# First chunks of the hidden layer with four weight blocks, and unit 0's rows of xT by DMA

## The chip, the cores and the metric

The kernel runs on one NeuronCore of a Trainium2 chip. The metric is device time in microseconds, lower is better. TensorE (PE) multiplies, VectorE (DVE), ScalarE (ACT) and GpSimd (POOL) work element by element, and SyncE (SP) issues most DMAs. Each engine runs its instructions in the order of the program and waits on semaphores for the others. 16 DMA engines move data between HBM and the on-chip memory (SBUF); matmuls write to PSUM.

## The reference

An RWKV6 attention is followed by a feed-forward layer. B, H, S, D = 4, 8, 768, 48; 3072 tokens, a model width of 384 and a hidden width of 2048. The two weight matrices are given in double precision.

```python
for t in range(S):
    cur = np.einsum('bhd,bhe->bhde', u[None] * kt, vt)
    y[:, :, t] = np.einsum('bhd,bhde->bhe', rt, state + cur)
    state = wt[:, :, :, None] * state + np.einsum('bhd,bhe->bhde', kt, vt)
...
x = np.ascontiguousarray(attn_out.transpose(0, 2, 1, 3)).reshape(B * S, H * D)
h = x @ w_in
sp = np.maximum(h, 0.0) + np.log1p(np.exp(-np.abs(h)))
g = h * erf(sp)
return (g @ w_out).astype(np.float32)
```

## The kernel before

**Steps and units.** Twelve steps s each take 128 tokens of two batches through the attention; the result of a step is a unit of 256 tokens for the feed-forward layer. Each step multiplies within its chunk by levels: at level n products of k and r (`level_products`, L728) are masked into the tile `own`, and VectorE then scales k and r by products of the decay w (`scale`, L375; L368 in step 0) before the next level. After six levels `from_own` (L772) and `through_state` (L798) sum y in PSUM. While the levels of step s run, PE fills the gaps with matmuls of earlier units: `hidden` (x @ w_in, L1289) and `project` (g @ w_out). `place` is called after each level and puts one piece of such work there. A piece of `hidden` is six matmuls of 256 columns (two chunks of 128 hidden columns, times three blocks of xT); a profile counts 12 records for them. A copy (L1298) takes each piece's result out of PSUM, from one of two buffers `ps_m`. So piece n + 2 can begin only when the copy of piece n is done.

**The three blocks of xT.** y has four groups of 128 partitions, each with two heads of 48 rows in halves of 64. 384 rows fit into three full blocks: groups 0 to 2 give rows 0 to 47 of each half, and the fourth group's 2 x 48 rows are spread, 16 by 16, over the spare rows 48 to 63 of the three blocks, which the text calls lanes. The fourth group is first copied to SBUF (`y3`, L807). For the steps from 1 on, the three groups are copied to xT (L828) and six small DMAs of 16 partitions carry y3's rows into the lanes (L834), three on SP's queue and three on ScalarE's. Step 0 is done otherwise: `hop` multiplies y3 with three constant matrices `apart` (L816, built at L1672 to L1678), which adds the rows to the lanes of y in PSUM, and ScalarE copies the sums to xT (L822). `hop` stands between the two halves of level 1's products in step 1.

**The weights.** They come as double-precision words and are made into single precision on the chip, two chunks at a time; number i means the i-th such pair, 0 to 7 for w_in. l(i) loads the words in two halves (`load`, L181), b(i) takes the high words on ScalarE (L291), r(i) the low ones (L299), h(i) shifts on VectorE (L308), and o(i) adds on GpSimd (L321). From pair 2 on, b(i) writes into the PSUM tile y, so it must wait for h(i - 1). The words have three buffers, so l(i) waits for r(i - 3). The loads share SP's queue with the inputs of the steps and are held back by hand. A copy of one column into the words' buffer (L274 on ScalarE, L276 on GpSimd) waits for something that is to come first, and the DMA waits for the copy. l(1) is opened by the totals of step 0, l(2) by `middle`, l(3) by y3, l(4) by the last block of xT. In step 1, h(i) stands on VectorE in front of the scaling at L375: `stages["h"](level + 1)`, then `scale(s, level)`.

**Order on the engines.** It is written by hand in `attend_first` (step 0) and `attend` (the others); ScalarE's copy `fence` (L781) stands between the two passes of `from_own`. In step 1, place 2 issues step 2's first input (L1720) and w. ScalarE multiplies that input by u (L452) before b(7), and copies level 6's products to `own` (L745) after r(7).

## Time and profile before

| what | us |
|---|---|
| runs of the kernel | 569.4 median of 3 (568.28 to 569.9) |
| the profiled execution | 567.75, with a span of 566.0 |
| PE busy in the span | 560.9 |
| VectorE, ScalarE, GpSimd busy | 453.0, 358.3, 241.4 |
| first three steps' waits of ScalarE for weight loads (L291) | 3.0 in 3 |
| shift products of `hop` (L816) | 1.56, from 22.19 |
| copies of unit 0 to xT (L822) | 0.90, from 23.91 |

All other times are microseconds from the start of the span in the profiled execution. An engine's line in the timeline gives start, duration, engine, line of the kernel, operation, tile written from tiles read, count, and in brackets the idle time ahead of it with what ended it. "PEld" is the loading of weights into the array, "SPq" and "ACTq" are DMA issues by those engines. The chain of waits is followed back from the last instruction, at each step to what released it.

### The profile page before, as it was taken

What the parts mean: (1) busy time and instruction counts of PE and PEld (TensorE: products, weight loads), DVE (VectorE), ACT (ScalarE), POOL (GpSimd) and SP (SyncE); (2) the same over time, 40 slices, a digit from 0 to 9 for tenths busy, and PEclk for the clock granted to TensorE, in tenths of its full rate; (3) what the DMA queues carried; (4) which work ended last, traced back from release to release, by engine and by line L of the source; (5) the groups of instructions that cost most, each with busy time, mean ns of one, the idle gap of its engine ahead of it and who ended that gap; (6) DMA issues with size and microseconds to landing.
All of it is one profiled execution on the core that took longest, in us unless ns stands there. A gap on an engine that the chain in (4) does not pass through costs nothing.

```text
span 566.0 us, 16708 instructions
## 1 busy us (share of the span) xinstructions
PE 560.9 (99%) x7316; PEld 500.7 (88%) x7316; DVE 453.0 (80%) x512; ACT 358.3 (63%) x495; POOL 241.4 (43%) x262
## 2 busy tenths in 40 slices
PE   9999999999999999999999999999999999999997
PEld 6788886588988998998998998998899899989997
DVE  8895986999899898898798789689689487477910
ACT  4687787556558858748757766765676771589500
POOL 3875482533885883393284185176072000000000
PEclk9999999999999999999999999999999999999999
DMA  7796753250434325153245135235232201000000
GB/s 268 231 329 212 252 195 127 120 155 3 148 122 133 111 94 150 26 182 134 43 149 181 34 137 187 40 115 166 48 112 85 47 9 35 3 2 0 29 29 28
DMA packets 54081, 63.24 MB, mean 112 GB/s; under 512 B 35160, under 2 KB 40568, under 8 KB 52984
## 3 DMA queue, kind: packets, MB, share of 16 engines
q1 hardware_dynamic: 53480, 61.98, 34.9%
q8 instruction: 57, 0.93, 0.7%
q10 hardware_dynamic: 528, 0.20, 0.2%
q14 instruction: 16, 0.13, 0.1%
HBM read 52.39 MB, written 8.69 MB: 108 GB/s over the span
## 4 chain that ended last, share of the span: by engine, by line
PE 96%; DMA 1%; DVE 1%; ACT 1%; issue 0%; SPq 0%; POOL 0%; DVEq 0%; ACTq 0%; POOLq 0%
PE m L1289 36%; PE m L1411 36%; PE c L1514 6%; PE pp L728 5%; PE m L1321 4%; PE y L772 2%; PE y L798 2%; PE pp L848 2%; DMA words<-in_moe_w_in 1%; PE m L1109 1%; PE pp L1189 1%; PE pp L1115 1%; PE c L1411 0%; DVE in L375 0%; PE pp L861 0%
## 5 line engine op out<-in xcount | busy, mean ns | idle before, releaser
L1289 PE MATMUL m<-xT,w_in_sb 128*128 128x256 f32 x960 | 214.0, 381 | 0.0
L1289 PEld LDWEIGHTS m<-xT,w_in_sb 128*128 128x128 f32 x960 | 180.3, 190 | 24.4
L375 DVE TENSOR_TENSOR in<-in,tot_sb 128x1024 f32<-128x1024 f32 (+1 forms) x55 | 77.5, 1410 | 6.3 <-PE pp L728 6.0
L1298 ACT COPY h<-m 128x512 f32<-128x512 f32 x80 | 46.2, 578 | 53.5 <-PE m L1289 53.2
L1411 PE MATMUL m<-mixed,h 128*128 128x192 f32 x320 | 56.7, 331 | 0.0
L1411 PE MATMUL m<-w_out_sb,h 128*128 128x192 f32 x320 | 56.1, 329 | 0.0
L1411 PEld LDWEIGHTS m<-mixed,h 128*128 128x128 f32 x320 | 51.8, 190 | 0.8
L1411 PEld LDWEIGHTS m<-w_out_sb,h 128*128 128x128 f32 x320 | 52.0, 190 | 0.5
L1411 PE MATMUL m<-w_out_sb,room 128*128 128x192 f32 x288 | 49.7, 326 | 0.0
L1411 PEld LDWEIGHTS m<-w_out_sb,room 128*128 128x128 f32 x288 | 47.3, 190 | 0.1
L530 POOL TENSOR_TENSOR words<-words,own 128x384 f32<-128x384 f32 x21 | 30.4, 1447 | 25.7 <-DVE words L561 13.0
L1249 ACT ACT_TABLE_LOAD x28 | 35.9, 1283 | 7.2 <-DVE h L1254 6.8
L728 PEld LDWEIGHTS pp<-in 48*48 48x48 f32 (+4 forms) x2368 | 30.2, 120 | 10.7 <-issue 5.3
L571 POOL TENSOR_TENSOR words<-words 128x384 f32<-128x384 f32 x28 | 38.7, 1411 | 0.0
L523 POOL TENSOR_TENSOR own<-rest 128x384 f32<-128x384 f32 x7 | 8.1, 1152 | 71.2 <-ACT o L1417 53.7
L1245 ACT ACT_TABLE_LOAD x28 | 35.9, 1283 | 1.8 <-issue 1.3
L728 PE MATMUL pp<-in 48*48 48x32 f32 (+4 forms) x2368 | 34.0, 206 | 0.1
L596 DVE TENSOR_REDUCE sums<-rk 128x16 f32<-128x768 f32 (+2 forms) x31 | 31.3, 1022 | 0.0
L475 POOL TENSOR_TENSOR tot_sb<-tot_sb 128x256 f32<-128x256 f32 (+4 forms) x50 | 29.7, 594 | 3.8
L571 POOL TENSOR_TENSOR rk<-words 128x384 f32<-128x384 f32 x28 | 30.6, 1120 | 0.0
L1245 ACT ACTIVATE room<-h 128x1024 f32<-128x1024 f32 x28 | 29.6, 1057 | 0.3
L321 POOL TENSOR_TENSOR w_out_sb<-w_out_sb,rest 128x768 int32<-128x768 int32 x8 | 17.1, 2142 | 22.3 <-DVE w_out_sb L313 22.2
(236 smaller groups left out, 1008.1 us busy)
## 6 DMA issues: line engine op xcount, KB each, us to landing
in<-in_rkw SPq DMA_DIRECT2D x8, 1024.0 KB, 5.3
words<-in_moe_w_in SPq DMA_DIRECT2D x16, 384.0 KB, 4.9
words<-in_moe_w_out SPq DMA_DIRECT2D x16, 384.0 KB, 4.8
words<-in_rk_rows SPq DMA_DIRECT2D x8, 768.0 KB, 5.9
w<-in_rkw SPq DMA_DIRECT2D x11, 512.0 KB, 8.8
v<-in_v SPq DMA_DIRECT2D x12, 384.0 KB, 5.7
out<-o SPq DMA_DIRECT2D x23, 192.0 KB, 3.9
in<-in_rkw SPq DMA_DIRECT2D x7, 512.0 KB, 5.0
```

Source lines behind the costliest of these rows:

```text
L375: nc.vector.tensor_mul(halves, halves, view(tots[level - 1], 0, [[1, n], [2, nb], [0, half]]))
L475: nc.gpsimd.tensor_mul(new, pair[:, :, 0], pair[:, :, 1])
L530: engine.tensor_mul(to, to, of[:, :, None, :].to_broadcast([P, NEAR // 2 // half, half, D]))
L571: engine.tensor_mul(to[:, i], r[:, half:], k[:, part * rows + i, None].to_broadcast([P, half, D]),)
L596: nc.vector.tensor_reduce(out=to, in_=of, axis=mybir.AxisListType.X, op=ALU.add)
L728: nc.tensor.matmul(to, lhsT=rk(1, n)[rows(e), s0 : s0 + m], rhs=right, start=True, stop=True,)
L1245: nc.scalar.activation(sp_room, chunks[0], AF.Softplus)
L1249: nc.scalar.activation(at, sp_room, AF.Erf)
L1289: nc.tensor.matmul(ps[:, ff, :], lhsT=w_in_sb[:, g * FG + f + ff, kk * P : (kk + 1) * P], rhs=xT[:, kk, :], start=kk == 0, stop=kk == KT - 1,)
L1298: nc.scalar.copy(h[:, f : f + FT, :], ps[:])
L1411: nc.tensor.matmul(to, lhsT=a[:, f], rhs=b[:, f], start=start and f == 0, stop=f == FG - 1, skip_group_check=True,)
L1514: nc.tensor.matmul(to[:, f], lhsT=turns["weights"][b][:, i * FT + f], rhs=turns["tokens"][a], start=a + b in STARTS and not f, stop=True, ...
```

## The change

**Unit 0's first piece** takes y's four groups as they are. x0 (in the free tile `room`) holds copies of groups 0 to 2, y3 the fourth. For the first two chunks the host sets the lane rows of w_in to zero and gives the rows that belong to y3 in a small array of their own, `w_lane`. So these two chunks are four matmuls each in place of three. `w_lane` is loaded behind l(0), converted in four stages beside those of the weights (ScalarE, VectorE, GpSimd), and later six DMAs on SP (`spread_lane`) put its rows into the lanes of the first two chunks of w_in, for the units that follow.

**Unit 0's xT**, for its other pieces, gets its lanes by the same six DMAs as in later steps. `hop` and `apart` are gone, and level 1 of step 1 is one run of products. The copies of y alternate between VectorE and ScalarE.

**The loads and conversions** move: l(1) opens after level 3's totals of step 0, l(2) where l(1) was, b(1) stands in front of the fence, r(1) behind the copies and DMAs of xT, l(3) is opened by a column of xT's block 1, l(4) by r(1). o(0) and o(1) are done in two halves.

```diff
+        def spread_lane():
+            n = D // KT
+            for kk in range(KT):
+                for e in range(NE):
+                    nc.sync.dma_start(
+                        out=weights[0][0][e * EP + D : (e + 1) * EP, :, kk * P : (kk + 1) * P],
+                        in_=lane_sb[e * EP + kk * n : e * EP + (kk + 1) * n],
+                    )
...
-        copy(y3[:].rearrange("p (j t) -> p j t", j=NJ), y[:, 1, 1])
-        if not s:
-            stages["l"](3, y3[:, 0:1], True)
...
-            def hop():
-                for kk in range(KT):
-                    nc.tensor.matmul(
-                        parts[kk], lhsT=apart[:, kk],
...
-                for kk in range(KT):
-                    nc.scalar.copy(by_kk[kk], parts[kk])
-                stages["l"](4, xT[:, KT - 1, 0:1], True)
...
+            nc.vector.tensor_copy(out=y3_of, in_=y[:, 1, 1])
+            nc.scalar.copy(x0_of[0], parts[0])
+            nc.vector.tensor_copy(out=x0_of[1], in_=parts[1])
+            nc.scalar.copy(x0_of[2], parts[2])
+            nc.vector.tensor_copy(out=by_kk[2], in_=parts[2])
+            for kk in range(2):
+                nc.scalar.copy(by_kk[kk], parts[kk])
+            turns["x0"] = [*(x0[:, kk] for kk in range(KT)), y3[:]]
...
@@ attend_first
             if level == 2:
                 stages["b"](0)
                 stages["r"](0)
+                turns["lane"][1]()
             if level == 3:
...
+                stages["l"](1, ready[0][1][3][:, 0:1])
             if level == LOG - 2:
-                stages["l"](1, ready[0][1][LOG - 1][:, 0:1])
+                stages["l"](2, ready[0][1][LOG - 1][:, 0:1])
...
         stages["h"](0)
+        stages["b"](1)
         state_of(0, halves[0], sums[0])
         from_own(0, own, 1)
         fence(nc.scalar.copy)
...
-        stages["l"](2, middle[:, JP - 1, 0:1], True)
+        turns["lane"][2]()
         stages["o"](0)
+        turns["lane"][3]()
         nc.gpsimd.tensor_mul(faded[1][:], middle[:], ends[:, :, 1:2].to_broadcast([P, JP, D]))
         through_state(0, xT)
-        stages["b"](1)
+        stages["l"](3, xT[:, 1, 0:1], True)
         stages["r"](1)
+        stages["l"](4, turns["last_rest"](1), True)
         stages["h"](1)
...
@@ attend
-                level_products(pp, rk, level, range(NP))
-                turns.pop("hop")()
-                level_products(pp, rk, level, range(NP, JP))
+                level_products(pp, rk, level)
...
@@ hidden
+                    if not of and not g + f:
+                        for kk, x in enumerate(turns["x0"]):
+                            nc.tensor.matmul(
+                                ps[:, ff, :],
+                                lhsT=(
+                                    w_in_sb[:, ff, kk * P : (kk + 1) * P] if kk < KT
+                                    else turns["w_lane"][:, ff]
+                                ),
+                                rhs=x, start=not kk, stop=kk == KT,
+                            )
+                        continue
...
         stages["l"](0)
+        turns["lane"][0]()
...
                     if (s, n) == (1, 2):
+                        turns["lane"][4]()
                         nc.sync.dma_start(out=loaded[2][0][:, 0], in_=rkw[2][:, 0])
```

The list `turns["lane"]` holds the five stages of the lane weights, in the order load, scale (two ScalarE instructions of 256 columns), shift (VectorE), add (GpSimd) and spread.

More of the change, by code (lines that the diff above doesn't have):

```diff
@@ L104 @@
     u_rows: bass.AP,
+    w_lane: bass.AP,
     out: bass.AP,
@@ L319, in add @@
             if i in held:
-                into = weights[i][0].bitcast(I32)
-                nc.gpsimd.tensor_tensor(
-                    out=into, in0=into, in1=held.pop(i)["rest"][:], op=ALU.add
-                )
+                into, rest = weights[i][0].bitcast(I32), held.pop(i)["rest"]
+                for part in (slice(0, 1), slice(1, 2)) if i < 2 else (slice(0, 2),):
+                    nc.gpsimd.tensor_tensor(
+                        out=into[:, part], in0=into[:, part], in1=rest[:, part], op=ALU.add
+                    )
         def join(i):
@@ L327, in join, with load_lane, scale_lane, shift_lane @@
             add(i)
+        lane_sb, low_sb = (
+            room[:, n, : 2 * P].rearrange("p (f m) -> p f m", f=2) for n in (1, 2)
+        )
+        turns["w_lane"] = lane_sb
+        def load_lane():
+            if plain:
+                nc.sync.dma_start(out=lane_sb, in_=w_lane)
+                return
+            words = wide.tile([P, 2, DM], I32, name="rest", bufs=2)
+            words = words[:].rearrange("p a b -> p (a b)")[:, : 4 * P]
+            nc.sync.dma_start(out=words, in_=w_lane.bitcast(I32).rearrange("p f m -> p (f m)"))
+            held["lane"] = words.rearrange("p (f m two) -> p f m two", f=2, two=2)
+        def scale_lane():
+            if "lane" in held:
+                words = held["lane"]
+                nc.scalar.activation(
+                    lane_sb, words[..., 1].bitcast(FP32), AF.Prelu, scale=2.0**-112, alpha=-(2.0**32)
+                )
+                nc.scalar.mul(
+                    out=low_sb.bitcast(I32), in_=words[..., 0].bitcast(U32), mul=2.0**-29
+                )
+        def shift_lane():
+            if "lane" in held:
+                nc.vector.tensor_scalar(
+                    out=lane_sb.bitcast(I32), in0=lane_sb.bitcast(I32), scalar1=3, scalar2=None,
+                    op0=ALU.logical_shift_left,
+                )
+        def add_lane():
+            if "lane" in held:
+                nc.gpsimd.tensor_tensor(
+                    out=lane_sb.bitcast(I32), in0=lane_sb.bitcast(I32), in1=low_sb.bitcast(I32),
+                    op=ALU.add,
+                )
+        def spread_lane():
[5 more added lines that the diff above has]
+                        in_=lane_sb[e * EP + kk * n : e * EP + (kk + 1) * n],
+                    )
+        turns["lane"] = load_lane, scale_lane, shift_lane, add_lane, spread_lane
         stages = {"l": load, "b": scale_high, "r": scale_low, "h": shift, "o": add, "j": join}
         done = {"l": 6, "b": 2, "r": 2, "j": NT // 2}
-        def last_rest():
-            return held[done["r"] - 1]["rest"][:, 0, 0:1]
+        def last_rest(i=None):
+            return held[done["r"] - 1 if i is None else i]["rest"][:, 0, 0:1]
         turns["last_rest"] = last_rest
@@ L806, in through_state @@
         copy = nc.vector.tensor_copy if s == 1 else nc.scalar.copy
-        copy(y3[:].rearrange("p (j t) -> p j t", j=NJ), y[:, 1, 1])
-        if not s:
-            stages["l"](3, y3[:, 0:1], True)
+        y3_of = y3[:].rearrange("p (j t) -> p j t", j=NJ)
         parts = y[:, 0, 0], y[:, 0, 1], y[:, 1, 0]
@@ L812, in through_state @@
         if not s:
-            def hop():
-                for kk in range(KT):
-                    nc.tensor.matmul(
-                        parts[kk], lhsT=apart[:, kk],
-                        rhs=y3[:].rearrange("p (j t) -> p j t", j=NJ),
-                        start=False, stop=True, skip_group_check=True,
-                    )
-                for kk in range(KT):
-                    nc.scalar.copy(by_kk[kk], parts[kk])
-                stages["l"](4, xT[:, KT - 1, 0:1], True)
-            turns["hop"] = hop
-            return
-        for kk in range(KT):
-            copy(by_kk[kk], parts[kk])
+            x0 = room[:, 0, : KT * UNIT].rearrange("p (k t) -> p k t", k=KT)
+            x0_of = [x0[:, kk].rearrange("p (j t) -> p j t", j=NJ) for kk in range(KT)]
+            nc.vector.tensor_copy(out=y3_of, in_=y[:, 1, 1])
[6 more added lines that the diff above has]
+            turns["x0"] = [*(x0[:, kk] for kk in range(KT)), y3[:]]
+        else:
+            copy(y3_of, y[:, 1, 1])
+            for kk in range(KT):
+                copy(by_kk[kk], parts[kk])
         by_scalar = {(kk, 1) for kk in range(KT) if s <= DIRECT}
@@ L1287, in hidden @@
                 for ff in range(FT):
+                    if not of and not g + f:
[7 more added lines that the diff above has]
+                                rhs=x, start=not kk, stop=kk == KT,
+                            )
+                        continue
                     for kk in range(KT):
@@ L1671 @@
         nc.vector.memset(t[:], 0.0)
-    apart = mixed[:].rearrange("p i f n -> p (i f n)")[:, : KT * P]
-    apart = apart.rearrange("p (k m) -> p k m", k=KT)
-    nc.vector.memset(apart, 0.0)
-    for kk in range(KT):
-        n = D // KT
-        to, of = (x.rearrange("p (e m) -> p e m", e=NE) for x in (apart[:, kk], ident[:]))
-        nc.vector.tensor_copy(out=to[:, :, D:], in_=of[:, :, kk * n : (kk + 1) * n])
     load_first()
@@ L1845 @@
             ]
+    w_pairs = moe_w_in[order].reshape(P, KT, DFF // P, P).transpose(0, 2, 1, 3)
+    w_pairs = np.ascontiguousarray(w_pairs)
+    w_lane = np.zeros((P, 2, P), moe_w_in.dtype)
+    for place in range(2):
+        rows = slice(place * EP, place * EP + D)
+        w_lane[rows] = moe_w_in[of[2 * q_last + (e_last ^ place), e_last], : 2 * P].reshape(D, 2, P)
+        w_pairs[place * EP + D : (place + 1) * EP, :2] = 0
     arrays = {
@@ L1852 @@
         "in_u": u_pad.reshape(2 * EP, NP),
-        "in_moe_w_in": as_given(
-            moe_w_in[order].reshape(P, KT, DFF // P, P).transpose(0, 2, 1, 3).reshape(P, -1, DM)
-        ),
+        "in_moe_w_in": as_given(w_pairs.reshape(P, -1, DM)),
         "in_moe_w_out": as_given(moe_w_out.reshape(DFF // P, P, DM).transpose(1, 0, 2)),
@@ L1861 @@
         "in_u_rows": np.ascontiguousarray(u_rows).reshape(P, D),
+        "in_moe_w_lane": as_given(w_lane),
     }
```

## The prediction

> **What bounds the kernel now.** I read the page first, then the chain of waits, then the timeline from 17 to 54 us, the only stretch that the change touches.

> ```profile
> span 566.0 us, 16708 instructions
> ...
> PE 560.9 (99%) x7316; PEld 500.7 (88%) x7316; DVE 453.0 (80%) x512; ACT 358.3 (63%) x495; POOL 241.4 (43%) x262
> ```

> TensorE is idle 5.1 us in all. So an edit can win no more than the PE work that it takes out plus a share of those 5.1 us, while every wait that it puts in front of PE is lost for good. The chain of waits says where such a wait is near:

> ```profile
> 24.00 0.82 ACT xT L822 x3
> ...
> 25.44 6.39 DMA words<-in_moe_w_in
> ...
> 31.93 0.89 ACT y L291
> ...
> 33.72 2.12 DVE in L375
> ...
> 35.89 1.03 PE pp L728 x64
> ```

> From 24 to 36 us the chain leaves PE. It runs from the last xT copy, which opens the fifth weight load l(4), through that transfer, ScalarE's conversion b(4), VectorE's shift h(4) (behind which the scaling L375 stands) to the level-4 products at 35.89. PE is still 95% busy in 34 to 36 us (1.90 of 2.00), so the cover is there, but it is about used up: whatever delays l(3) or l(4) shows at 35.89. The timeline has the parts:

> ```profile
> 21.04 0.66 PE L798 MATMUL y<-in,middle 48*48 48x64 f32 x32
> ...
> 21.76 0.37 ACT L807 COPY y<-y 128x256 f32<-128x256 f32 x1 [0.35 <-PE y L798]
> ...
> 22.19 1.56 PE L816 MATMUL y<-y,mixed 128*128 128x256 f32 x6
> ...
> 24.57 2.86 PE L1289 MATMUL m<-xT,w_in_sb 128*128 128x256 f32 x12
> 24.84 0.19 ACT L274 COPY words<-xT 128x1 f32<-128x1 f32 x1
> ...
> 28.95 0.88 ACT L291 ACTIVATE y<-words 128x768 f32<-128x768 f32 x1 [0.48 <-DMA words<-in_moe_w_in]
> ```

> Unit 0's y ends at 21.70 (I call this T0), the shift products follow, and piece 1 of the hidden layer runs from 24.57 to 27.43. ScalarE waits for loads at 28.95 and again at 31.93. The transfer sizes and times to landing in this stretch:

> ```profile
> xT<-y SPq DMA_DIRECT2D x3, 16.0 KB, 3.1
> xT<-y ACTq DMA_DIRECT2D x3, 16.0 KB, 2.1
> ```

> **PE's own work.** Out: three shift products, 1.56 us (L816), and the break they make in level 1, whose second half takes 0.96 us against 0.65 for the first: 0.3. In: two more matmuls in piece 1, 2.86 / 6 = 0.48 each: 0.95. Net -0.9 us. The constants for the products (L1674, three copies at L1678, 0.7 us of VectorE) go too; that time lay under PE's warm-up matmuls and is worth nothing.

> **The copies.** Four copies of y become seven, alternating VectorE and ScalarE, each waiting for the last (the listing of the changed program's waits: they read one PSUM tile). By 0.42 (VectorE, the y3 copy at 53.21) and 0.37 (L807) with 0.04 between them they end T0 + 2.95. PE sees only the first: level 1 runs unbroken to T0 + 1.0 (1.18 us for 64 products, as at 6.78, begun 0.19 before T0), x0's first chunk is there at T0 + 0.9, and each next one comes within a matmul's 0.48. The lane weights for the fourth block come from Pool: o(0) ends 22.82, plus a 256-wide add (0.6, L444), 23.4; they are needed at T0 + 2.4. Hidden, with 1 us to spare. Their conversion on ScalarE falls into its idle time at 12 to 13.4 us, VectorE's 0.4 us shift into the wait before T0. Uncovered, these would cost 0.4 to 0.6 us.

> **Loads 1 and 2 are opened earlier** (l(1) at level 3, about 14.6 instead of 17.38). DMA is 0.33 busy from 16 to 18 us, so there is room; the lane load (256 KB, 0.65 us at the 400 GB/s of 4 to 8 us) pushes everything behind it back by up to that. l(1) now lands behind w of step 1, at about 19.6 to 20.1. But its b(1) stands on ScalarE in front of the fence copy L781 (20.29), for which the second from_own products wait (20.59). Bounds: 0, if it landed by 19.2, to 2.5, if it landed only when b(1) could run before (22.26). I take 0.4: T0 is 22.1, and piece 1 runs 23.1 to 26.9, half a microsecond earlier than before.

> **Load 3 now waits for the rows of xT.** This is the step that decides. The gating copy L274 for l(3) reads chunk 1 of xT over all partitions, and the listing has it wait for both DMAs that write that chunk. xT[1] is copied at T0 + 2.95 = 25.05. ScalarE then issues three DMAs (0.61, then 1.50 for two, at 54.0), the second of them at 25.35. Landing takes 1.8 (the median at 140 us) to 3.1 (above); with empty queues I take 2.0, so 27.4. Until then ScalarE stands, with r(1), the gate of l(4), b(2) and all later conversions behind it, and DMA is idle from about 22. So l(3) is issued at 27.8 instead of 23.3. The like of it, l(1), alone on the queue, took 3.7 us for its first half; second half 0.4 later with 384 KB more: 4.4 together (bounds 3.9, as for the 512 KB at 39.35, and 5.2, as for l(3) before). It is there at 32.2 instead of 28.95, and l(4) 2.0 later at 34.2 instead of 31.83. [...]

> Then: r(1) 27.6 to 28.5; o(1) on Pool in halves of 0.9 from 28.5; piece 2 at 29.4 (29.13 before), level 3 to 33.3. b(3) 32.2 to 33.1, r(3) to 33.9, and only then on ScalarE the copy of piece 1's result (0.57) to 34.5, which frees the PSUM buffer of piece 3: piece 3 runs 34.5 to 37.3, PE having stood 1.2. b(4) 34.5 to 35.4, h(4) to 36.4, scaling (1.35 to 2.1, L375 at 40.69 and 33.72) to 38.1: level 4 starts at 38.1 instead of 35.89, PE having stood another 0.8. **+2.2 us**, the -0.9 and +0.4 included.

> **Six more DMAs on SP** (the lane rows into w_in) stand between l(7) and step 2's inputs.

> ```profile
> 34.58 0.36 SPq L1720 DMA_DIRECT2D in<-in_rkw  x1
> ...
> 40.22 1.32 ACT L452 ACTIVATE rk<-in,u_sb 128x128 f32<-128x128 f32 x4
> ...
> 44.32 1.17 ACT L745 COPY own<-pp 32x512 f32<-32x512 f32 x2
> ```

> l(7) goes behind r(4), to about 37.2; six issues at 0.62 (three took 1.87 at 53.99) make it 41.0; the input is issued there and, with 3.1 to 3.9 us to landing, is in at 44.6. ScalarE wants it at 40.22 + 2.4 = 42.6, stands 2.0, and 5.3 us later (44.32 + 1.17 - 40.22) has finished L745 at 49.9. PE wants that at 46.74 + 2.2 = 48.95: **+0.95**. Bounds: 0 if an issue costs 0.33 as for a load; 1.9 if landing takes 5.0, as at 34.58. Pool's totals and o(6) slip by 2 to 3 us as well, against 2.7 us of lead over piece 7.

> After 50 us PE is the bound again and nothing gives time back: +3.15. The profiled execution took 567.75 us (566.0 span and 1.75 around it) and would take 570.9. The median of the runs is 569.4, 1.65 above it; on that scale **572.5 us**. With the low ends (-0.4, -0.5, -0.95) the case goes down to 570.7, with the high ends (xT 1.1, l(3) 0.8, SP 0.9) to 575.4.

> **Rivals.**
> *The cover holds (not slower).* Place: 22 to 36 us. l(1) and l(2) are in by 22 us, two conversions are ahead, and the small DMAs land early, so that b(3) runs by 30.0; level 4 then starts no later than before. It decides from the point where l(3) is issued by 25.5. For it: DMA's gap at 16 to 18 is filled, and 0.1 us of PE's wait at 34 to 36 goes. Against: seven copies and two DMA issues before the gate put the issue at 25.7 even if landing took nothing. Price -0.9: 568.5.
> *The fence.* l(1) lands as late as 21.96 since v, w and the lane load are in front of it; b(1) then holds the fence until 22.9, PE's second from_own starts 2.4 later, not 0.4. For it: the load at 13.63 was still landing at 18. Against: 16 DMA engines a third busy at 16 to 18. Price +2: 574.5.
> *The clock.* The granted clock is 1.00 in each 2 us of this stretch, and PE never stands longer than 0.6 us in it. If my two waits (1.2 and 0.8, a whole piece between them) fell together with a longer one, the clock might fall; at half of it a piece and a level (2.86 + 1.03) would take 3.9 more: 576.4. [...]

> **Chances.** Forecast 0.61 (0.06 of it within 0.3% of 569.4), cover 0.27 (0.12 of it more than 0.3% faster, if waits go that I don't see), fence 0.09, clock 0.03. 0.3%, 1.7 us, is about what a measurement of this kernel can tell from no change. So faster 0.12, same 0.21, slower 0.67. The range 568.4 to 575.5 leaves out some 0.12 below and 0.06 above.

> **What would show it.** Right: ScalarE's wait for xT ending near 27.4; l(3) issued after it; the two waits of PE, before piece 3 and before level 4; ScalarE waiting at the first u product of step 2; piece 1 of 16 records ending before 27.4. Wrong: b(3) at 30 or sooner, or level 4 at 36 or sooner; or PE standing before T0, which would mean the fence.

## Result: slower, by almost three times what was forecast

The changed kernel takes 577.82 us (median of 4 runs, 577.2 to 578.48), the kernel before 568.93 beside it (4 runs, 568.28 to 569.9): 8.9 us more, a ratio of 1.0155, 95% interval 1.0134 to 1.0176. The forecast was 3.15 more. The profiled execution took 577.2, against 567.75 before. Code lines from L375 on are 48 to 60 higher than before (L728 is now L778, L1289 is L1349); those of the weights move by one or two (L291 is now L292).

The page's span and its first busy line, after:

```profile
span 575.4 us, 16739 instructions
...
PE 564.5 (98%) x7314; PEld 503.5 (88%) x7314; DVE 453.6 (79%) x512; ACT 359.0 (62%) x496; POOL 243.0 (42%) x266
```

TensorE now stands 10.9 us instead of 5.1, and is *busy* 3.6 us longer with 0.9 us less to do: part of its work ran at a lower clock. Where the time went, by the starts of the same work in the two timelines (us):

| start of | before | after | later by | forecast |
|---|---|---|---|---|
| T0, the end of unit 0's y | 21.70 | 23.37 | 1.67 | 0.4 |
| level 4 of step 1 | 35.89 | 41.07 | 5.18 | 2.2 |
| step 1's first own products (L772, L822) | 46.74 | 54.06 | 7.32 | 3.15 |
| the next piece of the hidden layer | 48.27 | 57.44 | 9.17 | 3.15 |
| end of the span | 566.0 | 575.4 | 9.4 | 3.15 |

The chain of waits, after (start, duration, what it was):

```profile
20.58 1.56 issue
...
26.80 3.42 DMA xT<-y
...
30.90 3.87 DMA words<-in_moe_w_in
...
38.86 2.17 DVE in L425
...
41.07 1.07 PE pp L778 x64
...
43.13 1.26 SPq L373
...
45.08 4.22 DMA in<-in_rkw
```

The forecast's links are all there: xT's DMA, load 3, VectorE's scaling, level 4, then SP's lane DMAs (L373) and the input of step 2. The first line was not forecast: 1.56 us in which TensorE waits for nothing that the profile shows. The timeline of the same kernel shows each place (start, duration, engine, line; in brackets the idle time before it and what ended it):

```profile
22.14 0.29 PE L1102 MATMUL pp<-v,kT 64*48 64x48 f32 x5 [1.56 <-issue]
...
26.14 0.48 PE L778 MATMUL pp<-rk 48*64 48x64 f32 x6 [1.35 <-issue]
26.55 2.93 PE L1339 MATMUL m<-room,w_in_sb 128*128 128x256 f32 x6
...
30.30 0.19 ACT L275 COPY words<-xT 128x1 f32<-128x1 f32 x1 [3.95 <-DMA xT<-y]
...
34.87 0.89 ACT L292 ACTIVATE y<-words 128x768 f32<-128x768 f32 x1 [1.73 <-DMA words<-in_moe_w_in]
...
49.33 1.31 ACT L502 ACTIVATE rk<-in,u_sb 128x128 f32<-128x128 f32 x4 [3.82 <-DMA in<-in_rkw]
...
54.06 0.32 PE L822 MATMUL y<-own,v 64*48 64x64 f32 x4 [2.06 <-ACT own L795]
...
55.68 1.97 PE L1238 MATMUL pp<-ident,in 128*128 128x128 f32 x8
```

The gate of load 3 ends its wait at 30.30 (forecast 27.4). Two matmul groups run at half speed: L1339's six take 2.93, where six before took 1.43 (half of the 2.86 that twelve of L1289 took), and L1238's eight 1.97, in the kernel before 1.09. The windows view gives the granted clock, the number in front of the DMA share:

```profile
24.00:26.00 2.00, 0.79 (x26) 0.60 (x20) 1.19 (x3) 1.02 (x4) 1.81 (x3) 0.50 0.00 0
...
54.00:56.00 2.00, 1.65 (x34) 1.36 (x35) 1.33 (x1) 1.17 (x3) 1.88 (x3) 0.57 0.91 270
```

**The stops.** Counting TensorE's weight loads, matmuls and semaphore instructions in the trace, the stop of 1.56 stands before number 962, that of 1.35 before number 1218: 256 apart. The trace has a DMA queue of its own for instructions (the page's "q8 instruction"). It carries packets of 16 KB, 57 of them for the 14 716 instructions that this count gives in the kernel before. These are the times of two packets, and when TensorE reaches the two numbers:

```
                    packet of 16 KB       number reached
kernel before       18.06 to 19.13        962 at 20.46, no stop
                    21.51 to 22.80        1218 at 24.19, no stop
kernel after        19.67 to 20.61        962 at 22.14, stop of 1.56
                    23.26 to 24.70        1218 at 26.14, stop of 1.35
```

Each number is reached 1.3 to 1.5 us after the end of its packet, with a stop in front of it or without. The first packet is late: it begins 2.67 us after TensorE reached number 706, against 1.14 in the kernel before. The second is not (1.12 after number 962, against 1.05): there TensorE uses its 256 instructions up in 2.65 us of running instead of 3.73.

That TensorE waits for its next 256 instructions is at this point a reading of times; the experiments test it.

### The profile page after: what moved, and what is told of

It reads as the page before. It is cut to its first block, busy times and chain, and to the rows that moved or that the text cites. A ratio compares the mean times of both kernels' runs of the same rounds, so it can differ in the third digit from the quotient of the medians.

```text
span 575.4 us, 16739 instructions
## 1 busy us (share of the span) xinstructions
PE 564.5 (98%) x7314; PEld 503.5 (88%) x7314; DVE 453.6 (79%) x512; ACT 359.0 (62%) x496; POOL 243.0 (42%) x266
## 3 DMA queue, kind: packets, MB, share of 16 engines
q1 hardware_dynamic: 54008, 62.39, 34.5%
## 4 chain that ended last, share of the span: by engine, by line
PE 93%; DMA 2%; DVE 1%; ACT 1%; issue 1%; SPq 1%; ACTq 0%; POOL 0%; DVEq 0%; POOLq 0%
PE m L1471 35%; PE m L1349 34%; PE c L1574 6%; PE pp L778 5%; PE m L1381 4%; PE y L822 2%; PE y L848 2%; PE pp L894 2%; PE m L1160 1%; PE pp L1238 1%; DMA in<-in_rkw 1%; DMA words<-in_moe_w_in 1%; PE pp L1166 1%; DMA xT<-y 1%; SPq L373 0%
## 5 line engine op out<-in xcount | busy, mean ns | idle before, releaser
L1349 PE MATMUL m<-xT,w_in_sb 128*128 128x256 f32 x948 | 211.4, 381 | 0.0
L1349 PEld LDWEIGHTS m<-xT,w_in_sb 128*128 128x128 f32 x948 | 178.2, 190 | 24.3 <-DMA xT<-y 0.3
L580 POOL TENSOR_TENSOR words<-words,own 128x384 f32<-128x384 f32 x21 | 30.4, 1447 | 25.7 <-DVE words L611 13.0
L778 PEld LDWEIGHTS pp<-in 48*48 48x48 f32 (+4 forms) x2368 | 30.2, 120 | 11.1 <-issue 5.6
L778 PE MATMUL pp<-in 48*48 48x32 f32 (+4 forms) x2368 | 33.9, 206 | 0.6 <-DVE in L425 0.6
```

The source lines that it names most:

```text
L580: engine.tensor_mul(to, to, of[:, :, None, :].to_broadcast([P, NEAR // 2 // half, half, D]))
L778: nc.tensor.matmul(to, lhsT=rk(1, n)[rows(e), s0 : s0 + m], rhs=right, start=True, stop=True,)
L1349: nc.tensor.matmul(ps[:, ff, :], lhsT=w_in_sb[:, g * FG + f + ff, kk * P : (kk + 1) * P], rhs=xT[:, kk, :], start=kk == 0, stop=kk == KT - 1,)
```

## Experiments

Each run is given with its ratio to the kernel before on the same chip.

### What do the early loads and the first stop cost?

**e1**, the kernel before with loads 1 and 2 opened early:

```diff
@@ kernel before
             if level == 3:
+                stages["l"](1, ready[0][1][3][:, 0:1])
             if level == LOG - 2:
-                stages["l"](1, ready[0][1][LOG - 1][:, 0:1])
+                stages["l"](2, ready[0][1][LOG - 1][:, 0:1])
```

> The kernel before, with one part of the change alone: l(1) opens after level 3's totals of step 0 and l(2) where l(1) was; b(1) stays where it was. Theory A (TensorE's instructions are fetched by DMA, 256 at a time, and the early loads hold the fetch up): TensorE stands about 1.5 us at 20.6 us in the middle of the L1054 products without a wait in the program, the fetch that began at 18.06 begins near 19.8; time 569 to 575, slower by 1 us or more. Theory B (the fence: b(1) in front of it holds the second pass of from_own): no wait at 20.6, since b(1) has not moved; time within 1 us of the kernel before, or faster, since l(2) and l(3) are in earlier.

569.48 us, ratio 0.9996 (0.997 to 1.0021). Early loads alone cost nothing on the whole, though the profiled execution has a stop of 0.73 at 18.07 (before number 706), half the clock behind it from 19.3 to 22.7 (L1047's eight matmuls take 1.82, the same eight in the kernel before 1.09), and a span 2.8 us longer than that of the kernel before. The stop of 1.5 at 20.6 that theory A named is not there.

**e2**, the changed kernel with loads 1, 2 and b(1) put back (the reverse of that diff, and b(1) behind `through_state`):

> The changed kernel with l(1), l(2) and b(1) put back where they were. Theory A: the first wait (1.56 us at 20.6) is gone, unit 0's y ends at 21.7 instead of 23.4. The second (1.35 us at 24.8) stays in part, 0.5 to 1.4 us, since level 1 without the shift products uses up 256 instructions in 2.7 us and a fetch takes about 4. If the clock was halved because of the first wait, it now stays whole until 50 us; time 572 to 574.5. Theory B: y ends at 21.7 too, but the wait at 24.8 has nothing to do with it and stays at 1.35; time 573 to 576.

577.24, 1.0123 (1.0098 to 1.0147). The packet comes at 17.83 instead of 19.67, the stop at 962 is gone and T0 is 21.88; the stop at 1218 stays, 1.59. But level 4 still starts at 40.38: load 3's gate opens at 29.27, still behind xT's DMAs, whose three issues on SP take 3.42 us here instead of 1.86. **e4** keeps the early loads and puts three wide matmuls, which bring few instructions for their time (12 in 1.43 us, by the 0.48 of one; 58 of level 1's products bring 116 in 1.09 in e2), in front of the first own products:

```diff
+        stay_warm(3)
         from_own(0, own, 1)
```

> The changed kernel with three warm-up matmuls of 256 columns (1.4 us, 12 instructions, their results are not used) in front of the first pass of from_own. Theory A with the clock: they run in the time in which TensorE would stand for its instructions, so the wait at 20.6 shrinks from 1.56 to 0.4 or less and y ends within 0.3 us of 23.4; if the wait is what halves the clock at 23.6, the clock stays whole and the kernel is 2 to 4 us faster. Rival (the clock falls because of the second wait or of the small products, not of the first wait): the clock is halved at 23.6 as before, time within 0.7 us of the changed kernel. Theory B: y ends 1.4 us later, slower by 1 to 1.5 us.

577.53, 1.0129 (1.0105 to 1.0154). The stop at 962 and the half clock before 50 us are gone here as well, and nothing is won. The filler holds TensorE as long as the stop did (T0 is 23.97), so what this run shows to be covered is the half clock. At full clock TensorE runs into the two waits that the forecast named, before piece 3 (forecast 1.2) and before level 4 (forecast 0.8): 0.96 and 1.18 in e4, 0.90 and 1.64 in e3 (below), and in e2:

```profile
36.33 2.83 PE L1349 MATMUL m<-xT,w_in_sb 128*128 128x256 f32 x12 [1.05 <-ACT h L1358]
40.38 1.03 PE L778 MATMUL pp<-in 48*56 48x32 f32 x64 [1.22 <-DVE in L425]
```

In the changed kernel's own profile the half clock takes most of their place: there is no wait before piece 3, and 0.57 before level 4.

e4 also shows that the second stop goes by the count of instructions. With 12 more ahead of it (the filler's six weight loads and six matmuls), it stands 12 instructions earlier in the program, behind 52 of level 1's products instead of 58, and again before number 1218:

```profile
26.00 0.45 PE L778 MATMUL pp<-rk 48*64 48x64 f32 x12 [1.21 <-issue]
```

### Gate and lane DMAs

**e3**, the changed kernel with the six lane DMAs behind step 2's inputs:

```diff
                     if (s, n) == (1, 2):
-                        turns["lane"][4]()
...
                         load_v(1)
+                        turns["lane"][4]()
```

> The changed kernel with the six DMAs of the lane rows behind step 2's inputs and v of step 1 instead of in front of them. If these six are what makes ScalarE stand 3.8 us for step 2's input and TensorE 2.1 us for own at 52, after which its clock is halved for 3.4 us: no wait at 52, no halved clock at 54 to 58, 4.1 us faster than the changed kernel, 573 to 574.5. Rival (the wait for the input comes from l(6) and l(7), which are late themselves): less than 1.5 us faster.

574.43, 1.0076 (1.0047 to 1.0105), 3.4 below the changed kernel. Level 4 is at 41.55, as late as in the changed kernel, but the own products follow without a wait and at full clock (timeline of e3):

```profile
41.55 1.03 PE L778 MATMUL pp<-in 48*56 48x32 f32 x64 [1.64 <-DVE in L425]
...
52.41 0.66 PE L822 MATMUL y<-own,v 64*48 64x64 f32 x32
53.12 1.09 PE L1238 MATMUL pp<-ident,in 128*128 128x128 f32 x8
```

**e5** takes the DMA wait alone out of load 3's gate:

```diff
-        stages["l"](3, xT[:, 1, 0:1], True)
+        stages["l"](3, turns["x0"][2][:, 0:1], True)
```

> Changed kernel, with the copy that opens load 3 reading the last chunk of x0 in place of xT[1], so that it waits for ScalarE's own earlier copy and no longer for the DMAs of xT. Gate theory (level 4's delay of 5.2 us is that of load 3, which waits for the rows of xT): load 3 is issued near 26.5 in place of 30.5, b(3) runs near 31, level 4 starts at 37 to 38.5 in place of 41.07, and the time falls by 2.5 to 3.5 us, to 574 to 575. Rival (TensorE is late by itself: the stops of 1.56 and 1.35 us in which it waits for nothing the profile shows, and the half clock after them, 3.4 us of work time at half speed): level 4 starts at 40 or later all the same and the time falls by less than 1 us.

577.12, 1.0121 (1.0083 to 1.0159). By the expectation this speaks against the gate, but it was a weak test of it: ScalarE issues three of xT's DMAs itself in front of the gate, and reached it at 30.59, after 2.37 of issuing. In this execution the stop at 962 was also longer, 2.52, and T0 came at 25.24; counted from T0, level 4 is 1.6 us sooner than in the changed kernel (table below). **e6** and **e7** add the late lane DMAs, and e7 the late loads too:

> As the run before, and the six lane DMAs stand on SP behind the inputs of step 2 (as in e3). Gate theory with the spread as a second and separate cost: the gains add, 3 and 3.4 us, giving 570 to 572. If the two waits cover each other (the spread DMAs are late only since load 7 is late), the gain of the second is under 1.5 us here, and the time is 573 to 574.

> As the run before, and loads 1 and 2 and the conversion b(1) are back where the kernel before has them, so that DMA has room for TensorE's instruction fetch at 18 to 20 us. If the gate and the spread were all, 570 to 572 as in e6 (the early loads gain or cost nothing). If, with the gate off the path, TensorE's own stop of 1.56 us now counts, this run is 1 to 2 us below e6: 569 to 570.5. If loads 1 and 2 are themselves needed early for level 4, it is 1 to 2 us above e6.

573.72, 1.0076 (1.0051 to 1.01), and 572.98, 1.0057 (1.0034 to 1.008): neither reaches its 570 to 572. e6 lies where the two waits covering each other would put it (573 to 574); the second mechanism looked for in e7, 1 to 2 us, is not outside the spread.

**e9** moves the gate to where the kernel before has it, ahead of the copies and the issues (and takes the line at xT out):

```diff
             nc.vector.tensor_copy(out=y3_of, in_=y[:, 1, 1])
+            stages["l"](3, y3[:, 0:1], True)
```

> Changed kernel, with load 3 opened by y3, ahead of the copies and of the DMAs of xT, as in the kernel before; all else as changed (the spread in front of step 2's inputs too). e5 did not test the gate: ScalarE itself issued three of xT's DMAs, and these issues held it until 29 to 30.5 just as the wait had. Gate theory (ScalarE's copies, issues and wait in front of load 3 are what delays level 4): load 3 is issued near T0 + 0.8 (about 24) in place of 30.5, b(3) runs before 31, level 4 starts at 38 or sooner, and the time is 2 to 3 us below the changed kernel, 574.5 to 575.5, the wait for step 2's inputs being left. Rival (the instruction fetch sets level 4): level 4 at 39.5 or later, time within 1 us of the changed kernel.

574.05, 1.009 (1.0057 to 1.0124). Level 4 is 2.6 us sooner in its profiled execution, the fastest of its five (572.36 to 578.42):

```profile
38.48 1.03 PE L778 MATMUL pp<-in 48*56 48x32 f32 x64 [0.85 <-DVE in L425]
```

**e10** has e9's edit and e3's, **e11** also issues all of xT's DMAs on SP:

```diff
-        by_scalar = {(kk, 1) for kk in range(KT) if s <= DIRECT}
+        by_scalar = {(kk, 1) for kk in range(KT) if 0 < s <= DIRECT}
```

> As the run before, and the six lane DMAs on SP behind the inputs of step 2. If gate and spread are separate costs, 571 to 572.5; what is then left over the kernel before is the two stops for instructions (1.3 to 1.7 us each) less the 0.9 us of TensorE work saved. If the spread was late only because the loads were, 573.5 or more.

> As the run before, and all six DMAs of xT are issued by SP: ScalarE goes on to r(1) and the gate of load 4 at once. If ScalarE's issues of 0.5 to 0.8 us each count, load 4 is issued 1 to 2 us sooner and the time is 0.5 to 1.5 us below e10. If load 4 waits on SP behind the six issues all the same, or TensorE is the bound by then, it is within 0.5 us of e10.

573.51, 1.0064 (1.0039 to 1.009), and 575.26, 1.0094 (1.0065 to 1.0123). e11 came out above e10, which neither of its forecasts names. Gate and lane DMAs are not separate costs: by the medians 3.8 and 3.4 alone, 4.3 together. The two gains added, by the ratios of e9 and e3, would leave a ratio of 1.001, outside e10's interval. They meet at the wait of 2.06, which e3 takes away and e9 cuts to about 0.4, and at the half clock behind it, which both take away. 4.6 us are left by the medians, 2.2 to 5.1 by e10's interval.

In e10's own profile, level 4 is later than in the changed kernel, in spite of the early gate:

```profile
42.10 1.03 PE L778 MATMUL pp<-in 48*56 48x32 f32 x64 [0.97 <-DVE in L425]
```

The stop at 962 was 2.78 us there. Counting from T0 separates the two causes (us, one profiled execution each):

| profile of | T0 | load 3's gate, from T0 | level 4, from T0 | level 4 |
|---|---|---|---|---|
| kernel before | 21.70 | 0.47 | 14.19 | 35.89 |
| changed kernel | 23.37 | 6.93 | 17.70 | 41.07 |
| e2 | 21.88 | 7.39 | 18.50 | 40.38 |
| e3 | 23.22 | 6.95 | 18.33 | 41.55 |
| e4 | 23.97 | 6.47 | 17.44 | 41.41 |
| e5 | 25.24 | 5.35 | 16.13 | 41.37 |
| e9 | 23.06 | 0.60 | 15.42 | 38.48 |
| e10 | 26.13 | 0.60 | 15.97 | 42.10 |

With the gate late, level 4 starts 17.4 to 18.5 us after T0; with the gate at y3, 15.4 and 16.0. So the gate is worth about 2 us at level 4, and the stop before T0 moves everything behind it. The last 1.2 to 1.8 us over the kernel before are not tested; load 4's gate, r(1), comes 5.7 and 6.3 us after T0 in e9 and e10, against 3.1.

### What is left, and what the shift products were worth

**e8** leaves the shift products out of the kernel before:

```diff
             def hop():
-                for kk in range(KT):
-                    nc.tensor.matmul(
-                        parts[kk], lhsT=apart[:, kk],
...
```

> Kernel before, with the three shift products left out (unit 0's output is then wrong in the fourth group's rows) and all else as it is: it measures what the removed TensorE work is worth. Work theory (TensorE is the bound, 1.56 us of products and the break of 0.3 go): 567.3 to 568, 1.5 to 2 us below the kernel before. Fetch theory (level 1 and piece 1 then use up the instructions faster than the fetch of the next 256 brings them): a stop of 1 us or more before about the 1218th TensorE instruction, inside piece 1, takes the place of the products, and the time is 568.8 to 569.4.

570.21, 1.0014 (0.9991 to 1.0038): no gain from 1.9 us less on TensorE. But ScalarE's b(1) and r(1) stand in front of xT's copies there, so piece 1 could hardly start sooner, and its profile has stops of 1.70 and 0.81 at 962 and 1218. **e16** broke level 1 by half of piece 1:

```diff
-                level_products(pp, rk, level, range(NP, JP))
+                level_products(pp, rk, level, range(NP, 6))
+                piece(hids, 0)
+                level_products(pp, rk, level, range(6, JP))
```

> e8 (kernel before with its three shift products left out) with the break of level 1 by the first half of piece 1. Fetch theory (the products' 1.56 us lay over the fetch, and without them TensorE stops as long): here the stop goes and the gain appears, 567 to 568, 2 us below e8. Rival (the products are hidden behind level 4's loads): as e8, 569 to 570.5.

573.18, 1.0063 (1.004 to 1.0087). It only met the late copies sooner and stood there; its profile also has a stop of 1.68 at 962 and half the clock from 23.7 to 30.5. **e17** puts the copies in front of the conversions, **e18** adds the break:

```diff
+            for kk in range(KT):
+                nc.scalar.copy(by_kk[kk], parts[kk])
+
             def hop():
```

> Kernel before without the three shift products (as e8), and ScalarE copies xT right behind y3, ahead of b(1) and r(1), so that nothing but TensorE's own instructions is left to hold piece 1. Fetch theory: the stop at 1218 is 1 to 1.8 us and piece 1 starts no more than 0.5 us sooner after T0 than the kernel before's 2.9: 568.3 to 569.5. Rival (the copies were all that held it): no stop over 0.4, piece 1 starts 1.4 us after T0, 567 to 567.8.

> As e17 with the first half of piece 1 behind 48 of level 1's 64 products. Fetch theory: the stop goes and the 1.5 us of TensorE work taken out show: 567 to 567.8, 1 to 1.7 us below e17. Rival: as e17 within 0.4 us.

e17: 570.12, 1.0025 (1.0002 to 1.0048). xT is copied by 23.3, and still TensorE stands inside level 1 (timeline of e17):

```profile
21.64 1.09 PE L728 MATMUL pp<-rk 48*64 48x64 f32 x58
...
24.59 0.34 PE L728 MATMUL pp<-rk 48*64 48x64 f32 x6 [1.86 <-issue]
24.86 4.54 PE L1284 MATMUL m<-xT,w_in_sb 128*128 128x256 f32 x12
```

The stop is again before number 1218, and as long as the products and their break were. In e18 it is gone:

```profile
25.08 0.46 PE L728 MATMUL pp<-rk 48*64 48x64 f32 x16
25.47 1.56 PE L1286 MATMUL m<-xT,w_in_sb 128*128 128x256 f32 x6
26.96 1.11 PE L728 MATMUL pp<-in 48*62 48x32 f32 x64
...
37.55 0.66 PE L728 MATMUL pp<-in 48*56 48x32 f32 x35 [1.46 <-DVE in L375]
```

Level 2 starts 4.44 after the end of y's last product (22.52), 5.66 in the kernel before: 1.2 won. Then level 4 stands 1.46 for the scaling behind loads 3 and 4, and the time is 569.79, ratio 1.0007 (0.9988 to 1.0025). The fetch theory was right on the stop and wrong on the gain: under the products lay the instructions, and under these the loads.

In the changed kernel, **e13** is e11 with the late loads, **e14** and **e15** break level 1 behind 48 of its 64 products (e14 on e13, e15 on e10):

```diff
-                level_products(pp, rk, level)
+                level_products(pp, rk, level, range(6))
+                piece(hids, 0)
+                level_products(pp, rk, level, range(6, JP))
```

> e11 (load 3 opened by y3, xT's six DMAs on SP, lane DMAs late) with loads 1 and 2 and b(1) back where the kernel before has them. Fetch theory: no stop at instruction 962, a stop of 1.3 to 2 us at 1218 remains; T0 near 22.1, level 4 near 37.5, time 571 to 572.5. Rival (waits for the loads make up what is left): level 4 at 39 or later with a wait for VectorE in front, 573 or more.

> As e13, and the first half of piece 1 (four matmuls of 0.48 us) stands behind 48 of level 1's 64 products, so that the next instructions can come while it runs. Fetch theory: no stop over 0.5 us at either place, 569 to 570.5, 1.5 to 2 us below e13. Rival: as e13 within 0.5 us, since level 4 waits for its loads and the stop was covered.

> e10 (loads 1 and 2 early) with the same break of level 1. Fetch theory: the stop at 962 stays (1.2 to 2.8 us), the one at 1218 goes: 571.5 to 572.5, 1 to 2 us below e10's 573.5 and 2 above e14. Rival: 573 to 574 as e10.

573.05, 1.0059 (1.0035 to 1.0082); 571.95, 1.0053 (1.004 to 1.0066); 573.41, 1.0077 (1.0061 to 1.0092). The fetch theory's forecasts all miss. e13 and e15 lie where their rivals put them (573 or more, 573 to 574), but e13 without the wait for VectorE that its rival named: TensorE stood 2.21 us for xT in front of piece 2. e14's profile has both stops under 0.5, and then others:

```profile
31.07 2.83 PE L1353 MATMUL m<-xT,w_in_sb 128*128 128x256 f32 x12 [1.09 <-DMA xT<-y]
...
38.83 0.44 PE L778 MATMUL pp<-in 48*56 48x32 f32 x17 [0.39 <-issue]
...
59.13 1.03 PE L778 MATMUL pp<-rk 48*64 48x64 f32 x50 [0.99 <-issue]
```

Piece 2 waits for the last rows of xT, and the stops at 38.83 and 59.13 come before numbers 1730 and 2498, three and six times 256 on from 962. Of the 4.6 us this names the kinds and gives no sum: how much is instructions and how much waits for xT and loads differs from profile to profile, and stays open.

**e12** asked whether such a stop also makes the kernel before vary (567.8 to 573.9 over all its runs here), with load 1 opened 1.3 us later:

```diff
-                stages["l"](1, ready[0][1][LOG - 1][:, 0:1])
...
+        stages["l"](1, ready[0][1][LOG - 1][:, 0:1], True)
```

> Kernel before, with load 1 opened 1.3 us later (by ScalarE, behind its copy at 17.9, in place of Pool at 16.8). Fetch theory (in some executions the fetch of TensorE's next 256 instructions, due at 17.4 to 17.8, falls behind load 1's 768 KB and TensorE stops for 1 to 2 us): the fetch now always goes first, no stop at instruction 962, the times above 570 go and the median is 567.9 to 568.6. Rival (the spread of the times has another cause, and load 1 is needed as early as it is): the same spread, median 568.9 to 570.

568.63, 0.9997 (0.998 to 1.0014), with runs up to 571.61: the theory is not borne out. No version measured beats the kernel before.

## Why the prediction was wrong, by its steps

**Right.** Slower; the stretch from 24 to 36 us as the bound; the second wait at step 2's input; and load 3's gate behind xT as a step that costs, though of the 5.2 us at level 4 the experiments give it about 2. The seven copies ended at T0 + 2.97 (forecast 2.95). From load 3's issue to b(3) it took 4.36 (4.4). The input landed 4.2 us after its issue, a little over the 3.1 to 3.9. In the chances, 0.67 stood on slower, but the range ended at 575.5.

**The signs named.** ScalarE's wait for xT ended at 30.30, not near 27.4; piece 1 ended at 32.1, not before 27.4; of the two waits of TensorE only the one before level 4 came, 0.57 (both are there in e2 to e4, at full clock). TensorE did stand before T0, which was to mean the fence; it meant the instructions.

**Four terms were too small.** With what they measured along the chain of the one profiled execution, +3.15 becomes 9.1 of the 9.4 by which the profiled spans differ. They are not what undoing each would win:

- *T0, +1.3.* "DMA is 0.33 busy from 16 to 18 us, so there is room": there was room for the loads. What they pushed back was TensorE's instructions, a transfer that the sum did not have (the packet of 18.06 began at 19.67); with the loads late (e2) T0 is 21.88. It moved the start of the copies, and so the gate. Undoing it alone won little: in e2 T0 is 1.5 sooner, load 3's gate 1.0 and level 4 0.7, and its time (576.16 to 577.49) overlaps the changed kernel's (577.2 to 578.48).
- *xT's landing, +1.4.* "With empty queues I take 2.0, so 27.4". The trace of after has 3.42 from that chunk's issue on, above even the 3.1 of the row for SP, though DMA was idle (a share of 0.00 from 24 to 26 us, the row quoted above). These two, and 0.2 at the issue, are the 3.0 missing at level 4.
- *The lane DMAs, +1.2.* Priced at 3.7 us, they held SP for 5.2, on top of the late load 7: the input was issued at 45.08, not 41.0, and TensorE stood 2.1 us, not 0.95 (7.32 - 5.18).
- *The clock, +1.85.* From 54.3 to 57.7 TensorE ran at half clock (9.17 - 7.32). I gave this rival 3 in 100, for waits of 1.2 and 0.8 that would have to fall together. That the clock would halve was my estimate, which no view of the kernel before shows (1.00 throughout the stretch); the changed kernel's trace has 0.50 for 3.41 us here. One wait of 2.06 was enough here, as were 2.43, 2.12 and 1.89 at the same place in e2, e4 and e5. e3 has no wait there, and no half clock.

**The credit of 0.9 us** for less work on TensorE was worth nothing from the start. e17 and e18 show why, in the kernel before: at that place TensorE needs the time for its own instructions (the stop of 1.86 in e17), and what it wins is given back at level 4, where load 4's chain, named in the prediction as the bound, sets the start. The rival "the cover holds", -0.9, could not have come out so.

**The rivals.** The fence was not the cause: b(1) began at 20.27, the fence copy followed at 21.09, and TensorE stood for instructions until 22.14 in any case (in e11, where load 1 landed later, the fence held TensorE 0.41). The clock came as a part, not as the case.

## What to carry to other kernels

When a load's gate is moved behind a small DMA, price the whole stretch: every issue on the gating engine and the slowest landing of the like in the trace (here 3.4 us, and 2.4 us of issuing once the wait was gone), and look at what the next queue entries then push back. Work taken off the bounding engine is worth only what is left when the next cover is reached: ask what ran under it, here the engine's own instructions and then a weight load. Two late steps that feed one wait are not added: undo each alone and both together before a cost is put on either. And where a stop shifts a whole stretch from one execution to the next, count from the start of the stretch (here T0), not from the start of the span.

## What the hardware showed unexpectedly

**TensorE stood where its next packet of instructions had only just landed.** 1.56 and 1.35 us in the changed kernel, 1.86 in e17, 2.78 in e10, before numbers that lie a multiple of 256 instructions apart (962 and 1218 in these; 706, 1730 and 2498 in others). The kernel before has no such stop, but next to no slack either: it reaches the two numbers 1.3 and 1.4 us after their packets of 16 KB, and the changed kernel's stops end 1.5 and 1.4 us after theirs. Long matmuls between many short ones took a stop away (e4 the one of 1.56, e18 that of 1.86), and moving two loads did too (e2).

```profile
20.13:23.54 3.41, 1.85 (x119) 1.72 (x111) 1.45 (x4) 1.18 (x3) 2.56 (x4) 1.00 0.47 171
50.85:54.26 3.41, 1.35 (x10) 0.84 (x8) 2.22 (x2) 3.35 (x7) 3.33 (x5) 1.00 0.43 141
23.54:30.37 6.83, 5.48 (x62) 4.45 (x54) 4.08 (x6) 1.47 (x5) 2.27 (x3) 0.50 0.07 17
54.26:57.67 3.41, 3.12 (x41) 2.87 (x38) 1.07 (x1) 0.94 (x2) 3.17 (x6) 0.50 0.93 338
```

The four changes at 23.54, 30.37, 54.26 and 57.67 are 6.83, 23.89 and 3.41 us apart, two, seven and one times 3.41. The mean granted clocks of the profiled executions, 1.000, 0.997, 0.994 and 0.991 to within 0.001, are what none, one, two and three stretches of 3.41 us at 0.50 give in 570 us. The length of a stop does not decide alone: in e3 a stop of 1.64, in e9 one of 1.52 and in e7 one of 1.87 left the clock at 1.00 (a mean of 1.000 in each), while in e1 it fell after one of 0.73 (0.997). TensorE was busy for 1.85 and 1.35 of the 3.41 us ahead of the two falls. What makes the clock fall stays open: in e3, 1.76 us busy of the 3.40 from 38.80 to 42.20 left it at 1.00.
